# Low words of the weights converted on GpSimd in the first batch

## The chip, the core and the metric

The kernel runs on one core of a Trainium2 chip. A core has five engines with queues of their own: TensorE (PE, the matrix products; PEld is its loading of weights), VectorE (DVE), ScalarE (ACT), GpSimd (POOL) and SyncE (SP, which here only starts transfers). They wait for each other through semaphores. Products go to PSUM, everything else lies in SBUF. The metric is the time of one execution on the device, in microseconds (us), the median of several runs.

## The reference

A two-sided attention between 512 tokens `x` and 32 states `state`, for 8 batches and 8 heads of depth 64, and behind it a two-layer network over the 4,352 rows that come out of it:

```python
scores = scale * x @ state^T;       a  = softmax(scores)    # over the 32 states
xread  = a @ state
scores2 = scale * state @ x^T;      a2 = softmax(scores2)   # over the 512 tokens
sread  = a2 @ x
y = concatenate([xread, sread], axis=2)       # (8, 8, 544, 64), then as rows of 512
h = y @ w_in                                  # 512 -> 2048
g = where(h >= 1, h, where(h <= -1, 0, (h + 1)**2 / 4))
out = g @ w_out                               # 2048 -> 512
```

## The kernel before

**Precision.** Large products run in a reduced fp32 type, so each operand is split into a high and a low part and a product is three passes of PE (high by high, low by high, high by low: lines 477 to 479 and 534 to 536). The weights are laid out by the caller in pieces of 1 MB: eight of `w_in` (called i0 to i7) and eight of `w_out` (o0 to o7). In the core's memory a piece is a tile of 128 x 1024 pairs of 32-bit words, a low word and a high word side by side (`raw_i`, `raw_o`). Three steps make a float of a pair: `high` (line 588, always ACT) converts the high words in place, `low` (lines 575 and 580) the low words in place, and `join` (line 596, always DVE) shifts one and ors the other in. The join of a piece of `w_in` gives `w32_c` (w in the profile). The join of a piece of `w_out` gives `wf`, of which `part_high` (line 603, ACT) and `part_low` (line 607, DVE) make the two parts `wo`.

**Work of a batch.** For a batch: the scores (line 253) into PSUM, `sc`; the softmax over states on DVE and ACT (transposes at line 260, maximum 271, subtraction 275, exponential 280, sum 284, division 288 to 293, transpose back 300), split into `ath` and `atl`; the softmax over tokens (maximum 318, exponential 322 into `e`), its transposes on PE (line 333, `e2p`), the copy of them back by ACT (line 337) and `sread` (line 350, `sr`, scaled into `rs`, then turned by PE in line 364 into `rt`). Since `xread` only feeds `w_in`, the states are multiplied into `w_in` first: `sw` (line 417) of a piece of `w_in`, split by ACT (line 432, `sw_h`) and DVE (line 436, `sw_l`). A block j of 256 hidden values is then `h` (lines 477 to 479), relu by ACT (482), square (485), a bound by DVE (488), its split into `gh` (497, ACT) and `gl` (502, DVE), and the accumulation into `acc` with piece j of `w_out` (lines 534 to 536). Eight blocks make a batch; after eight batches the states' own rows follow.

**Order.** From the second batch on the code is written in the order in which it is to run. The first batch is different: all weights have still to be loaded and converted in it, beside its own products. Its steps go to a planner, `Plan`, as `op(key, engine, cost, run, after, take, ends)`: what a step costs on an engine, what it comes behind, which buffer it takes or frees. `Plan.times` plays the steps through with these costs, the step with the longest way to the end first, and `emit` writes them out in the order in which they then began. So a cost is no more than a number that sets the order. A step whose engine reads "ACT/DVE" goes where it would end sooner. `LATE` is how long after a step's end another engine may see it. Where PE would idle between the first scores and the first accumulation, `emit` puts in warming products (`warm`, line 198) of the identity by itself; `WARM` of them stand ahead of the first scores. Each weight product of 128 x 128 in full fp32 shows as two records in the trace.

**Buffers.** Two `raw` tiles serve all pieces of `w_in` (a piece's transfer waits for the join of the piece two before), while each piece of `w_out` has a tile. One PSUM tile, `mm`, serves `sw`, `e2p`, `sr` and `rt` in turn; one tile `u` holds a block's hidden values until `gl` is made. For the first batch, xt is loaded, and its scores are made, in two halves of 256 tokens, with the state's first slice on ACT's queue beside it. SP's queue holds, in this order: xt of batch 0, i0, i1, o0, the other states, xn of batch 0, i2, o1, xt of batch 1, i3, o2, and so on.

Of the kernel before, what the change touches and what calls it, by code (L numbers as in the profile page):

```python
# [14 lines left out]
AX = mybir.AxisListType  # L15
PSUM = bass.MemoryType.PSUM

WARM = 10
PAD = 120
BIAS = {}  # L20

# [1 line left out]
class Plan:  # L23
# [1 line left out]

    LATE = {"SP": 3.9, "PE": 0.3, "ACT": 0.12, "DVE": 0.12}

    def __init__(self, room, turns, bias):  # L30
        self.bias = bias
# [5 lines left out]
    def op(self, key, engine, cost, run, after=(), take=(), ends=()):  # L37

        after = list(after)
        prior = self.last.get(engine) if engine in ("PE", "SP") else None  # L40
        self.last[engine] = key
        self.ops[key] = [engine, cost, run, after, list(take), list(ends), prior]

    def late(self, k):
        return self.LATE[self.ops[k][0].split("/")[0]]

# [32 lines left out]
    def times(self):  # L79
# [6 lines left out]
        free = dict(self.room)  # L86
        begun, done, where, idle = {}, {}, {}, {e: 0.0 for e in self.LATE}
        events = set()
# [49 lines left out]
def state_exchange_moe(  # L138
# [17 lines left out]
    nc = tc.nc  # L156
# [38 lines left out]
    def warm(n):  # L195

        for _ in range(n):
            nc.tensor.matmul(warmed[:, :P], lhsT=ident, rhs=ident, start=True, stop=True)  # L198
# [254 lines left out]
    class Hidden:  # L453
# [39 lines left out]
        def high(self):  # L493
            b, j = self.b, self.j
            gh = work.tile([P, 2, S], F32R, tag="gh", name=f"gh{b}_{j}")
            gl = work.tile([P, 2, S], F32R, tag="gl", name=f"gl{b}_{j}")
            nc.scalar.copy(out=gh, in_=self.u)  # L497
            gs[b, j] = (gh, gl)

        def low(self):  # L500
            gh, gl = gs[self.b, self.j]
            nc.vector.tensor_tensor(out=gl, in0=self.u, in1=gh.bitcast(F32), op=ALU.subtract)  # L502
# [68 lines left out]
    def low(kind, c, engine):  # L571

        lo = raws[kind, c][..., 0]
        if engine == "DVE":
            nc.vector.tensor_scalar(
                out=lo, in0=lo.bitcast(U32), scalar1=0.875 * 2.0 ** -29, scalar2=0.49,
                op0=ALU.mult, op1=ALU.add,
            )
        else:
            nc.scalar.activation(  # L580
                out=lo, in_=lo.bitcast(U32), func=AF.Relu, scale=0.875 * 2.0 ** -29, bias=offset
            )
# [7 lines left out]
    def join(kind, c):  # L590
        raw = raws[kind, c]
        if kind == "i":
            a = w32[c].rearrange("p k f -> p (k f)")
        else:
            a = parts[c] = work.tile([P, 1024], F32, tag="tmp", name=f"wf{c}")
        nc.vector.scalar_tensor_tensor(  # L596
            out=a.bitcast(I32), in0=raw[..., 1], scalar=3, in1=raw[..., 0],
            op0=ALU.logical_shift_left, op1=ALU.bitwise_or,
        )

    def part_high(c):
        wo[c] = wop.tile([P, 2, 2, DM], F32R, tag="wo", name=f"wo{c}")
        nc.scalar.copy(out=wo[c][:, 0].rearrange("p a c -> p (a c)"), in_=parts[c])  # L603

    def part_low(c):
        wh, wl = (wo[c][:, i].rearrange("p a c -> p (a c)") for i in range(2))
        nc.vector.tensor_tensor(out=wl, in0=parts[c], in1=wh.bitcast(F32), op=ALU.subtract)  # L607
# [5 lines left out]
    op = plan.op  # L613

    def read(key, cost, f, *a, take=(), after=()):
        op(("dma",) + key, "SP", cost, lambda: f(*a), after=after, take=take)

    def load(key, f, b):
        loaded[key, b] = f(b)

    def chunk_ops(c):

        k = ("i", c)
        read(k, 2.6, fetch, "i", c, take=[("raw", k)])
        op(("high",) + k, "ACT", 1.05, lambda: high("i", c), [("dma",) + k])
        op(("low",) + k, "ACT/DVE", (1.15, 0.75), lambda e: low("i", c, e), [("dma",) + k])
        op(("w", c), "DVE", 1.14, lambda: join("i", c), [("high",) + k, ("low",) + k], ends=[k])

    def out_ops(c):

        k = ("o", c)
        read(k, 2.6, fetch, "o", c)
        op(("high",) + k, "ACT", 1.05, lambda: high("o", c), [("dma",) + k])
        op(("low",) + k, "ACT/DVE", (1.15, 0.75), lambda e: low("o", c, e), [("dma",) + k])
        op(("join", c), "DVE", 1.14, lambda: join("o", c), [("high",) + k, ("low",) + k], take=[("tmp", k)])
        op(("woh", c), "ACT", 0.95, lambda: part_high(c), [("join", c)], ends=[k])
        op(("wol", c), "DVE", 1.14, lambda: part_low(c), [("woh", c)], ends=[k])
# [63 lines left out]
    def tensor(key, cost, f, after=(), take=(), ends=()):  # L701
        op(key, "PE", cost, f, after, take, ends)
# [31 lines left out]
    guard = tc.manual_schedule()  # L734
    nc.scalar.dma_start(out=sb[:, 0], in_=state[:, 0])
    read(("xt", 0, 0), 1.3, load, "xt", load_xt, 0, take=[("xt", ("xt", 0))])
    read(("xt", 0, 1), 1.3, lambda: None)
    chunk_ops(0)
    chunk_ops(1)
    out_ops(0)  # L740
    read(("sb", 1), 1.2, lambda: nc.sync.dma_start(out=sb[:, 1:], in_=state[:, 1:]))
    read(("xn", 0), 2.6, load, "xn", load_xn, 0, take=[("xn", ("xn", 0))])
    chunk_ops(2)
    out_ops(1)
    read(("xt", 1), 2.6, load, "xt", load_xt, 1, take=[("xt", ("xt", 1))])
    for c in range(3, NC):
        chunk_ops(c)
        out_ops(c - 1)
        if c == 5:
            read(("xn", 1), 2.6, load, "xn", load_xn, 1, take=[("xn", ("xn", 1))])  # L750
    out_ops(NC - 1)

    op(("table",), "ACT", 1.3, lambda: nc.scalar.copy(out=pad[:, :1], in_=half))
    tensor(("warm",), 4.5, lambda: warm(WARM))
    for side in range(2):
# [113 lines left out]
```

## Time and profile before

| | |
|---|---|
| median of 3 runs | 663.77 us (663.58 to 663.95) |
| span of the profiled execution | 662.2 us; the median of the runs is 1.6 us above it |
| PE busy | 653.9 us, 99% of the span |
| weight loads | 514.2 us, 78% |
| DVE | 340.3 us, 51% |
| ACT | 356.5 us, 54% |
| GpSimd | 0.8 us, seven instructions at the start |
| transfers | 43.65 MB, most of the weights' in the first 60 us |

The page has no other time of the profiled execution than its span. Busy time of PE is no measure of how near it is to its peak, since products overlap; what counts is where it waits. DVE, ACT and the transfers are busiest in the first batch, up to some 95 us, so stretches of it are read one by one.

### The profile page before, as it was taken

The page shows a single profiled execution, that of the slowest core. Times are in us where ns is not written, and L with a number is a line of the kernel's source. Part 1 is how long each engine was busy: PE and PEld are TensorE (multiplying, and loading weights), DVE is VectorE, ACT ScalarE, POOL GpSimd, SP SyncE. Part 2 cuts the span into 40 slices and gives each one's busy share as a digit, 9 for nine tenths or more (in the row PEclk, how much of TensorE's full clock was granted, in tenths as well). Part 3 has the DMA queues.
Part 4 walks back from the last instruction along what each step waited for, and adds up shares of the span by engine and source line. Part 5 has one row for each costly group of instructions (what it writes and reads, how often), then busy time and mean ns, then how long its engine had stood idle before and what let it go on. Part 6 is the DMA issues. An engine that isn't in the chain of part 4 may idle for free.

```text
span 662.2 us, 10304 instructions
## 1 busy us (share of the span) xinstructions
PE 653.9 (99%) x4442; PEld 514.2 (78%) x4442; DVE 340.3 (51%) x490; ACT 356.5 (54%) x462; POOL 0.8 (0%) x7
## 2 busy tenths in 40 slices
PE   8999999999999999999999999999999999999997
PEld 6677777777787777777787777777778777778896
DVE  5999947623673239433563338433563343333431
ACT  4899847544554446544554447444653454454642
POOL 0000000000000000000000000000000000000000
PEclk9999999999999999999999999999999999999999
DMA  8986103010301003010301002010100000000101
GB/s 359 400 359 249 64 10 119 0 65 0 120 10 64 1 4 124 0 65 0 128 1 64 1 24 105 0 65 0 65 1 1 1 33 32 1 1 1 63 1 33
DMA packets 11085, 43.65 MB, mean 66 GB/s; under 512 B 1312, under 2 KB 1440, under 8 KB 7968
## 3 DMA queue, kind: packets, MB, share of 16 engines
q1 hardware_dynamic: 6096, 34.28, 13.6%
q10 hardware_dynamic: 4944, 8.72, 3.5%
q8 instruction: 35, 0.57, 0.3%
q14 instruction: 10, 0.08, 0.0%
HBM read 34.08 MB, written 8.91 MB: 65 GB/s over the span
## 4 chain that ended last, share of the span: by engine, by line
PE 91%; ACT 5%; DVE 3%; issue 0%; DMA 0%; POOL 0%; SPq 0%; ACTq 0%; POOLq 0%
PE acc L534 19%; PE acc L536 18%; PE acc L535 18%; PE h L477 9%; PE h L479 9%; PE h L478 9%; PE sw L417 5%; PE sc L253 1%; PE sr L350 1%; PE e2p L333 1%; PE warmed L198 1%; ACT u L482 1%; ACT u L485 1%; ACT raw_i L588 1%; DVE w L596 1%; ACT wo L603 0%
## 5 line engine op out<-in xcount | busy, mean ns | idle before, releaser
L534 PE MATMUL acc<-wo,gh 128*128 128x512 f32 x544 | 218.8, 402 | 0.0
L535 PE MATMUL acc<-wo,gh 128*128 128x512 f32 x544 | 212.3, 390 | 0.0
L536 PE MATMUL acc<-wo,gl 128*128 128x512 f32 x544 | 212.2, 390 | 0.0
L482 ACT ACTIVATE u<-h,half 128x512 f32<-128x512 f32 x136 | 93.7, 693 | 219.9 <-PE h L479 202.6
L488 DVE SCALAR_TENSOR_TENSOR u<-u,h 128x512 f32<-128x512 f32 x136 | 87.0, 680 | 206.7 <-ACT u L485 206.7
L534 PEld LDWEIGHTS acc<-wo,gh 128*128 128x128 f32 x544 | 102.1, 188 | 40.1 <-ACT u L482 12.8
L536 PEld LDWEIGHTS acc<-wo,gl 128*128 128x128 f32 x544 | 102.1, 188 | 22.5 <-issue 0.4
L535 PEld LDWEIGHTS acc<-wo,gh 128*128 128x128 f32 x544 | 102.2, 188 | 19.4 <-DVE wo L607 0.3
L502 DVE TENSOR_TENSOR gl<-u,gh 128x1024 fp32r<-128x1024 f32 x68 | 83.2, 1224 | 33.0 <-ACT gh L497 32.0
L497 ACT CAST gh<-u 128x1024 fp32r<-128x1024 f32 x68 | 71.8, 1056 | 50.3 <-DVE u L488 49.9
L485 ACT ACTIVATE u<-u 128x1024 f32<-128x1024 f32 x68 | 72.5, 1065 | 1.3
L417 PE MATMUL sw<-w,sb 64*32 64x256 f32 x1024 | 36.0, 383 | 1.8 <-DVE w L596 1.3
L417 PEld LDWEIGHTS sw<-w,sb 64*32 64x32 f32 x1024 | 15.1, 106 | 17.9 <-issue 8.8
L479 PE MATMUL h<-atl,sw_0h 128*128 128x512 f32 x60 | 23.6, 393 | 0.3 <-DVE atl L306 0.2
L477 PE MATMUL h<-ath,sw_0h 128*128 128x512 f32 x60 | 23.5, 394 | 0.0
L549 ACT COPY o<-acc 128x512 f32<-128x512 f32 x33 | 18.6, 586 | 9.1 <-PE acc L536 9.0
L478 PE MATMUL h<-ath,sw_0l 128*128 128x512 f32 x60 | 23.5, 391 | 0.0
L479 PE MATMUL h<-atl,sw_6h 128*128 128x512 f32 x60 | 23.4, 389 | 0.0
L479 PE MATMUL h<-atl,sw_2h 128*128 128x512 f32 x60 | 23.4, 389 | 0.0
L477 PE MATMUL h<-ath,sw_2h 128*128 128x512 f32 x60 | 23.3, 389 | 0.0
L478 PE MATMUL h<-ath,sw_2l 128*128 128x512 f32 x60 | 23.3, 389 | 0.0
L477 PE MATMUL h<-ath,sw_4h 128*128 128x512 f32 x60 | 23.3, 389 | 0.0
(174 smaller groups left out, 735.0 us busy)
## 6 DMA issues: line engine op xcount, KB each, us to landing
xt<-in_xt_dram SPq DMA_DIRECT2D x16, 512.0 KB, 4.5
raw_i<-in_moe_w_in_dram SPq DMA_DIRECT2D x8, 1024.0 KB, 6.9
raw_o<-in_moe_w_out_dram SPq DMA_DIRECT2D x8, 1024.0 KB, 9.4
xn<-in_x_dram SPq DMA_DIRECT2D x8, 1024.0 KB, 6.4
out_dram<-o ACTq DMA_DIRECT2D x32, 256.0 KB, 2.0
sb<-in_state_dram SPq DMA_DIRECT2D x1, 448.0 KB, 12.6
out_dram<-o SPq DMA_DIRECT2D x4, 64.0 KB, 1.7
out_dram<-o ACTq DMA_DIRECT2D x4, 64.0 KB, 2.0
```

The source lines that it names most:

```text
L417: nc.tensor.matmul(pt[pr * NS:(pr + 1) * NS, hh, i * CI:(i + 1) * CI], lhsT=sb[rows, b, pr], rhs=w32[c + i][rows, pr], start=True, stop=True,)
L477: nc.tensor.matmul(o, lhsT=wh[:, k, sl], rhs=ah[:, k], start=first, stop=False)
L478: nc.tensor.matmul(o, lhsT=wl[:, k, sl], rhs=ah[:, k], start=False, stop=False)
L479: nc.tensor.matmul(o, lhsT=wh[:, k, sl], rhs=al[:, k], start=False, stop=last)
L482: nc.scalar.activation(out=self.u[:, i], in_=self.hs[i], func=AF.Relu, scale=0.5, bias=half)
L485: nc.scalar.activation(out=self.u, in_=self.u, func=AF.Square)
L488: nc.vector.scalar_tensor_tensor(out=self.u[:, i], in0=self.u[:, i], scalar=1.0, in1=self.hs[i], op0=ALU.min, op1=ALU.max,)
L497: nc.scalar.copy(out=gh, in_=self.u)
L502: nc.vector.tensor_tensor(out=gl, in0=self.u, in1=gh.bitcast(F32), op=ALU.subtract)
L534: nc.tensor.matmul(a, lhsT=lh, rhs=oh, start=f == 0, stop=False)
L535: nc.tensor.matmul(a, lhsT=lh, rhs=ol, start=False, stop=False)
L536: nc.tensor.matmul(a, lhsT=ll, rhs=oh, start=False, stop=f == NF - 1)
```

## The change

The low words of i2 to i7 and o2 to o7 are converted by GpSimd, with the instruction that DVE used; those of i0, i1, o0 and o1 stay with ACT or DVE. The planner is told 1.7 for such a step, and 0.2 as GpSimd's delay. Eight warming products stand ahead of the first scores instead of ten, and the planner takes the second half of xt to be there 0.6 earlier.

```diff
-WARM = 10
+WARM = 8
...
-    LATE = {"SP": 3.9, "PE": 0.3, "ACT": 0.12, "DVE": 0.12}
+    LATE = {"SP": 3.9, "PE": 0.3, "ACT": 0.12, "DVE": 0.12, "POOL": 0.2}
...
         lo = raws[kind, c][..., 0]
-        if engine == "DVE":
-            nc.vector.tensor_scalar(
+        if engine != "ACT":
+            (nc.vector if engine == "DVE" else nc.gpsimd).tensor_scalar(
                 out=lo, in0=lo.bitcast(U32), scalar1=0.875 * 2.0 ** -29, scalar2=0.49,
                 op0=ALU.mult, op1=ALU.add,
             )
...
+    def low_op(kind, c):
+        k = (kind, c)
+        if c < 2:
+            op(("low",) + k, "ACT/DVE", (1.15, 0.75), lambda e: low(kind, c, e), [("dma",) + k])
+        else:
+            op(("low",) + k, "POOL", 1.7, lambda: low(kind, c, "POOL"), [("dma",) + k])
...
-        op(("low",) + k, "ACT/DVE", (1.15, 0.75), lambda e: low("i", c, e), [("dma",) + k])
+        low_op("i", c)
...
-        op(("low",) + k, "ACT/DVE", (1.15, 0.75), lambda e: low("o", c, e), [("dma",) + k])
+        low_op("o", c)
...
-    read(("xt", 0, 1), 1.3, lambda: None)
+    read(("xt", 0, 1), 0.7, lambda: None)
```

The planner orders the first batch anew. On PE the order of products stays, and the numbers of warming products change: 8 instead of 10 ahead of the first scores, none instead of 2 between the halves of the scores, 18 instead of 16 behind them, 10 instead of 8 ahead of the transposes `e2p` of batch 0.

Three places follow; in each, the row in brackets names the engines that an instruction waits for. First DVE, around the first scores. Before (`sc0_0` and `sc0_1` are the two halves of the heads, `z0` the transposed scores; the first two transposes are those of the first 256 tokens, the other two those of the second 256):

```order
L260 STREAM_TRANSPOSE z0_120<-sc0_0_118 128x256 [waits PE_49]
L260 STREAM_TRANSPOSE z0_120<-sc0_1_119 128x256 [waits PE_49]
L271 TENSOR_REDUCE m1_0_121<-z0_120 128x8 [waits DVE_49] x2
L260 STREAM_TRANSPOSE z0_120<-sc0_0_118 128x256 [waits PE_49]
L260 STREAM_TRANSPOSE z0_120<-sc0_1_119 128x256 [waits PE_49]
L271 TENSOR_REDUCE m1_0_121<-z0_120 128x8 [waits DVE_49] x2
L275 TENSOR_TENSOR z0_120<-z0_120,m1_0_121 128x512 [waits DVE_49]
```

DVE at the same place in the changed kernel:

```order
L260 STREAM_TRANSPOSE z0_118<-sc0_0_116 128x256 [waits PE_49]
L260 STREAM_TRANSPOSE z0_118<-sc0_1_117 128x256 [waits PE_49]
L260 STREAM_TRANSPOSE z0_118<-sc0_0_116 128x256
L271 TENSOR_REDUCE m1_0_119<-z0_118 128x8 [waits DVE_49] x2
L260 STREAM_TRANSPOSE z0_118<-sc0_1_117 128x256
L275 TENSOR_TENSOR z0_118<-z0_118,m1_0_119 128x512 [waits DVE_49]
L271 TENSOR_REDUCE m1_0_119<-z0_118 128x8
L271 TENSOR_REDUCE m1_0_119<-z0_118 128x8 [waits DVE_49]
```

The third transpose has moved ahead of the maxima, and the transposes of the second half have no wait for PE of their own any more.

Second ACT, from the second split of the first softmax to the copy of the turned exponentials. Before (`ath0` is the split, `e2_0` the exponentials over tokens, `u0_0` and `h0_0` block 0 of batch 0, `sw0_1h` the high part of sw 1):

```order
L303 CAST ath0_116<-zt0_200 128x512 [waits DVE_49]
L322 ACTIVATE e2_0_237,sum2_0_239<-sc0_0_118,nm2_0_238 128x512 [waits DVE_49,Activation_49]
L482 ACTIVATE u0_0_222<-h0_0_0_223,half_78 128x512 [waits PE_49]
L482 ACTIVATE u0_0_222<-h0_0_1_229,half_78 128x512 [waits PE_49]
L432 CAST sw0_1h_262<-sw0_1_253 128x512 [waits PE_49]
L485 ACTIVATE u0_0_222<-u0_0_222 128x1024 [waits Activation_49]
L322 ACTIVATE e2_0_237,sum2_0_239<-sc0_1_119,nm2_0_238 128x512 [waits DVE_49]
L588 ACTIVATE raw_i2_198<-raw_i2_198 128x1024 [waits DMAHW0_49]
L497 CAST gh0_0_306<-u0_0_222 128x1024 [waits DVE_49,Activation_49]
L603 CAST wo0_310<-wf0_247 128x1024
L337 COPY e2_0_237<-e2p0_286 128x1024 [waits PE_49,Activation_49]
```

ACT there in the changed kernel:

```order
L303 CAST ath0_114<-zt0_198 128x512 [waits DVE_49]
L588 ACTIVATE raw_i2_192<-raw_i2_192 128x1024 [waits DMAHW0_49,Activation_49]
L482 ACTIVATE u0_0_220<-h0_0_0_221,half_78 128x512 [waits PE_49]
L482 ACTIVATE u0_0_220<-h0_0_1_227,half_78 128x512 [waits PE_49]
L432 CAST sw0_1h_261<-sw0_1_252 128x512 [waits PE_49]
L485 ACTIVATE u0_0_220<-u0_0_220 128x1024 [waits Activation_49]
L322 ACTIVATE e2_0_235,sum2_0_237<-sc0_0_116,nm2_0_236 128x512 [waits DVE_49]
L322 ACTIVATE e2_0_235,sum2_0_237<-sc0_1_117,nm2_0_236 128x512 [waits DVE_49]
L603 CAST wo0_279<-wf0_247 128x1024
L497 CAST gh0_0_301<-u0_0_220 128x1024 [waits DVE_49,Activation_49]
L337 COPY e2_0_235<-e2p0_292 128x1024 [waits PE_49,Activation_49]
```

The high words of i2 have moved from behind the second exponential to the front, and the first exponential from the front to behind the square. On DVE the join of i2 now stands where its low conversion stood, ahead of `sw0_1l`, and the low part of o0 (line 607) ahead of `gl` of block 0.

Third ACT at block 3 of batch 0, from `gh` of block 2 to the square. Before (`e2_1` are the exponentials of batch 1, `u0_3` block 3, `sw0_4h` the high part of sw 4):

```order
L497 CAST gh0_2_529<-u0_2_424 128x1024 [waits DVE_49,Activation_49]
L322 ACTIVATE e2_1_517,sum2_1_519<-sc1_487,nm2_1_518 128x512 [waits DVE_49,PE_49]
L322 ACTIVATE e2_1_517,sum2_1_519<-sc1_487,nm2_1_518 128x512 [waits DVE_49]
L588 ACTIVATE raw_o4_436<-raw_o4_436 128x1024 [waits DMAHW1_49]
L482 ACTIVATE u0_3_532<-h0_3_0_533,half_78 128x512 [waits DVE_49,PE_49,Activation_49]
L432 CAST sw0_4h_562<-sw0_4_553 128x512 [waits PE_49]
L482 ACTIVATE u0_3_532<-h0_3_1_543,half_78 128x512
L588 ACTIVATE raw_i6_499<-raw_i6_499 128x1024 [waits DMAHW3_49]
L485 ACTIVATE u0_3_532<-u0_3_532 128x1024 [waits Activation_49]
```

ACT there in the changed kernel:

```order
L497 CAST gh0_2_510<-u0_2_428 128x1024 [waits DVE_49,Activation_49]
L588 ACTIVATE raw_o4_440<-raw_o4_440 128x1024 [waits DMAHW1_49]
L322 ACTIVATE e2_1_525,sum2_1_527<-sc1_494,nm2_1_526 128x512 [waits DVE_49,PE_49]
L322 ACTIVATE e2_1_525,sum2_1_527<-sc1_494,nm2_1_526 128x512 [waits DVE_49]
L482 ACTIVATE u0_3_537<-h0_3_0_538,half_78 128x512 [waits DVE_49,PE_49,Activation_49]
L588 ACTIVATE raw_i6_489<-raw_i6_489 128x1024 [waits DMAHW3_49,Pool_49]
L482 ACTIVATE u0_3_537<-h0_3_1_550,half_78 128x512 [waits PE_49]
L432 CAST sw0_4h_570<-sw0_4_561 128x512 [waits PE_49]
L485 ACTIVATE u0_3_537<-u0_3_537 128x1024 [waits Activation_49]
```

The cast of sw 4 now stands behind i6's high words and the second relu, and o4's high words have moved ahead of the exponentials. GpSimd's queue holds the twelve conversions in the order i2, i3, o2, i4, o3, i5, o4, i6, o5, i7, o6, o7, each waiting for its transfer. SP's order is the same up to o5; xt of batch 2, which stood ahead of i7, now stands behind o7.

## The prediction

> **What bounds the kernel now.** I read the stretches first (columns: stretch, length, busy time of PE, PEld, DVE, ACT and POOL, granted clock, DMA share, GB/s), then TensorE's list of waits, then the timeline around the places that these name.
>
> ```profile
> 13.00:20.00 7.00, 6.13 (x50) 4.58 (x50) 6.93 (x14) 5.65 (x7) 0.00 (x0) 1.00 1.02 416
> 20.00:30.00 10.00, 8.85 (x74) 6.07 (x73) 9.62 (x16) 8.85 (x14) 0.00 (x0) 1.00 0.98 397
> 30.00:40.00 10.00, 10.00 (x116) 7.53 (x115) 9.73 (x13) 10.00 (x12) 0.00 (x0) 1.00 0.83 315
> 40.00:50.00 10.00, 9.98 (x72) 6.86 (x68) 9.03 (x14) 9.19 (x14) 0.00 (x0) 1.00 1.00 420
> 50.00:60.00 10.00, 10.00 (x70) 7.32 (x71) 9.62 (x12) 10.00 (x13) 0.00 (x0) 1.00 0.97 377
> 60.00:70.00 10.00, 9.86 (x61) 7.39 (x59) 9.96 (x15) 10.00 (x13) 0.00 (x0) 1.00 0.05 20
> ```
>
> From 30 us on PE has next to no idle time, and nothing behind the first batch is touched: the time is the moment at which the first batch hands over, plus fixed work. Ahead of 30 us PE waits. There DVE works 6.93 of 7.00 and 9.62 of 10.00 us, the transfers run at a share of 1.02 and 0.98, and from 30 to 70 us DVE and ACT are both nearly full. So this is a chain through DVE, ACT and transfers up to 30 us, and a race that PE only just wins up to 70 us. GpSimd does nothing.
>
> ```profile
> PE sw L417 <- DVE w L596: 1.3, 1, 1.3
> ```
>
> This is the longest wait of PE behind its start, and warming products fill most of the rest; a gain there must come from the chain that the fillers cover.
>
> **The scores (two warming products less).**
>
> ```profile
> 0.73 0.42 ACTq L735 DMA_DIRECT2D sb<-in_state_dram  x1
> 0.74 0.87 SPq L217 DMA_DIRECT2D xt<-in_xt_dram  x2
> 1.45 4.34 PEld L198 LDWEIGHTS warmed<-ident 128*128 128x128 f32 x20 [1.45 <-POOL ident masks.py:199]
> 6.01 1.11 PE L253 MATMUL sc<-xt,sb 64*32 64x256 f32 x16
> 7.21 0.78 DVE L260 STREAM_TRANSPOSE z<-sc 128x256 f32<-128x256 f32 x2 [6.31 <-PE sc L253]
> 7.73 0.97 PE L253 MATMUL sc<-xt,sb 64*32 64x256 f32 x16
> 8.04 0.18 PEld L253 LDWEIGHTS sc<-xt,sb 64*32 64x32 f32 x14 [0.18 <-DVE z L260]
> 8.78 0.78 DVE L260 STREAM_TRANSPOSE z<-sc 128x256 f32<-128x256 f32 x2 [0.16 <-PE sc L253]
> 10.11 0.68 DVE L275 TENSOR_TENSOR z<-z,m 128x512 f32<-128x512 f32 x1
> DMA to landing us min/median/max: 4.3/4.3/4.3
> DMA to landing us min/median/max: 4.2/4.6/5.0
> ```
>
> Twenty weight loads, two to a product, take 4.34 us: 0.43 a product, 0.87 for two. The first half of the scores could start at 6.01 - 0.87 = 5.14. The state lands at 0.73 + 4.3 = 5.03, the first half of xt at 0.74 + 4.2 = 4.94, so that holds. The half takes 7.05 - 6.01 = 1.04 (the four fillers behind it begin at 7.05, 0.16 ahead of the transposes at 7.21) and ends at 6.2, when the second half of xt lands (issued at about 1.2, 5.0 later). The two fillers between the halves are gone too. Before, the second half waited for the first transposes (row at 8.04); now it follows at once and ends at 7.24.
>
> But DVE's order (shown above for both) has the transposes of the first half wait for PE and those of the second half for nothing: the one wait covers both halves. They start 0.16 behind the second half, at 7.40. The eight instructions ahead of the first subtraction then run without the gap of 0.16: 10.11 - 7.21 - 0.16 = 2.74, up to 10.14 against 10.11. **Term: 0.0.** Bounds: -0.75, if the transposes start behind the first half, at 6.4, and keep a gap; +0.2, if the second half of xt lands that much later. After that DVE has the same instructions up to the first join of w_out, so sw and the softmax of batch 0 stay where they are.
>
> **Piece 2 of w_in, and what stands behind it on ACT.**
>
> ```profile
> 13.79 0.33 SPq L568 DMA_DIRECT2D raw_i<-in_moe_w_in_dram  x1
> DMA to landing us min/median/max: 6.8/6.8/6.8
> 21.15 0.69 ACT L322 ACTIVATE e<-sc,nm 128x512 f32<-128x512 f32 x1 [1.94 <-DVE nm L319]
> 21.83 1.26 ACT L482 ACTIVATE u<-h,half 128x512 f32<-128x512 f32 x2
> 23.60 0.69 DVE L436 TENSOR_TENSOR sw_1l<-sw,sw_1h 128x512 fp32r<-128x512 f32 x1
> 24.39 0.70 ACT L322 ACTIVATE e<-sc,nm 128x512 f32<-128x512 f32 x1
> 25.06 1.20 ACT L588 ACTIVATE raw_i<-raw_i 128x1024 f32<-128x1024 f32 x1
> 25.24 0.66 PE L333 MATMUL e2p<-ident,e 128*128 128x128 f32 x4 [0.24 <-ACT e L322]
> ```
>
> Piece 2 is issued at 13.79 and lands 6.8 later, at 20.6; with a DMA share of 1.02 it can't land earlier. ACT's conversion of its high words (1.20, of which the next instruction overlaps some 0.1) stood behind both second exponentials; it now stands ahead of the relus of block 0 and waits for that landing: 20.6 to 21.7. The relus started at 21.83, behind an exponential that had waited 1.94 for DVE: no loss. But both exponentials now come behind relus, cast and square. From 21.83 to 24.39 is 2.56, so the first starts at 24.26, the second 0.68 later (21.15 to 21.83), at 24.94, where it stood at 24.39. PE's second half of the transposes, 25.24 before, and block 1 behind it come 0.55 later.
>
> ```profile
> 27.99 1.04 ACT L337 COPY e<-e2p 128x1024 f32<-128x1024 f32 x1
> 29.09 0.67 PE L417 MATMUL sw<-w,sb 64*32 64x256 f32 x16 [0.45 <-ACT e L337]
> 30.17 0.19 PEld L535 LDWEIGHTS acc<-wo,gh 128*128 128x128 f32 x1 [0.30 <-DVE wo L607]
> ```
>
> That loss is covered: behind block 1 PE waited 0.45 for ACT's copy of the turned exponentials, and then 0.30 for the low part of w_out 0. The copy started 3.60 behind the second exponential (24.39 to 27.99); one conversion, 1.1, has left that stretch, so it starts at 24.94 + 3.60 - 1.1 = 27.44, and 0.55 earlier than before. The product sw_2 starts at 29.09 - 0.45 + 0.55 = 29.2 (+0.1). The low part of w_out 0 now stands ahead of gl on DVE, so the 0.30 goes; some of it may come back as a wait for gl, so I keep a **term of -0.2**. Bounds: -0.75, if the exponentials aren't later and both waits go; +0.55, if nothing covers.
>
> GpSimd's first conversion has to be over before DVE's join of piece 2, which stands ahead of sw_1l:
>
> ```profile
> 1.10 0.29 POOL masks.py:199 TENSOR_SCALAR_AFFINE_SELECT ident<-ident 128x128 f32<-128x128 f32 x1
> L575 DVE TENSOR_SCALAR raw_i<-raw_i x6: 684/686/690, 10.7 to 61.5; 128x1024 int32<-128x1024 uint32 x6
> ```
>
> No row has GpSimd on such a tile. Its select over 128 elements took 0.29; eight times that, 2.3, is the upper bound, DVE's 0.69 for the same instruction the lower. I take 1.7, nearer the row of its own engine. The Trainium skill ("GPSIMD Engine Reference", section 7) has about 1.9 cycles an element for such strides, an estimate of 1.6 us at 1.2 GHz; no run here shows it, and the sum would be the same. From 20.65 it ends at 22.4. DVE comes to the join at 23.60 - 0.69 = 22.9, where its own low conversion stood, spends 1.2 on it, and sw_1l ends at 24.7: still ahead of the first exponential's end at 24.95. **Term: 0**, cover 0.25 us.
>
> **Relief, and a new stall.** Seven conversions of 0.69 leave DVE (nine before, two left) and five leave ACT. PE hardly waits from 30 to 60 us, so by themselves they are worth nothing. One place gets worse, ACT's order at block 3:
>
> ```profile
> 48.98 1.18 DVE L502 TENSOR_TENSOR gl<-u,gh 128x1024 fp32r<-128x1024 f32 x1
> 50.82 0.70 ACT L482 ACTIVATE u<-h,half 128x512 f32<-128x512 f32 x1
> 51.40 0.61 ACT L432 CAST sw_4h<-sw 128x512 fp32r<-128x512 f32 x1
> 52.35 0.68 DVE L436 TENSOR_TENSOR sw_4l<-sw,sw_4h 128x512 fp32r<-128x512 f32 x1
> 53.39 0.27 PE L364 MATMUL rt<-ident,rs 128*128 128x128 f32 x1
> ```
>
> PE reaches rt at 53.39 and needs the buffer that sw_4l frees at 52.35 + 0.68 = 53.03: a margin of 0.36. ACT's cast sw_4h stood straight behind the first relu; now that relu, piece 6's high words (1.1) and the second relu (0.58, as 50.82 to 51.40) are ahead of it, 1.7 later. The first relu itself comes earlier: it needs gl, over at 50.16, and a conversion that held it until 50.82 has moved ahead of the exponentials: -0.65. Net 1.05 late: **+0.7** behind the margin (bounds 0 and +1.3). A like order stands at block 4, where PE idles 0.14 between 60 and 70 us now; 0 to 1.1, and I take **+0.1**, since ACT has been relieved by then. On SP's queue xt of batch 2 goes behind i7, o6 and o7; it is used after the first batch, the transfers end near 60 us (share 0.05 behind it): nothing, and the three pieces come earlier.
>
> **Sum.** 0.0 - 0.2 + 0.7 + 0.1 = +0.6. The profiled span is 662.2 us, 1.6 below the runs' median of 663.77; I add the difference to the median: **664.4 us**. About 0.2% (1.3 us) is what a measurement of this kernel can tell from no change, so this is no change. Its own range: 663.2 to 665.4.
>
> **Rivals.**
>
> 1. *DVE and GpSimd hinder each other: slower.* DVE's busiest groups between 28 and 62 us:
>
> ```profile
> L596 DVE SCALAR_TENSOR_TENSOR wf<-raw_o 128x1024 int32<-128x1024 int32 x5 | 6.1, 1217 | 0.0
> L607 DVE TENSOR_TENSOR wo<-wf,wo 128x1024 fp32r<-128x1024 f32 x5 | 6.1, 1214 | 0.0
> L596 DVE SCALAR_TENSOR_TENSOR w<-raw_i 128x1024 int32<-128x1024 int32 x4 | 4.9, 1217 | 0.0
> L502 DVE TENSOR_TENSOR gl<-u,gh 128x1024 fp32r<-128x1024 f32 x4 | 4.8, 1210 | 0.0
> ```
>
> Eighteen instructions with two SBUF inputs take 21.9 of 34 us, and eleven of the twelve GpSimd conversions fall here. A GpSimd instruction of 1.7 us always meets one. If each stops DVE for half its length, DVE loses 11 x 0.85 = 9.4 us, gets back 6 x 0.69 = 4.1 (those of the seven that stood here) and has 1.6 idle from 30 to 60 us: 3.7 late, and PE with it, its margin at rt being 0.36: 668.1. At full length it is 18.7 - 5.7 = 13.0, 677.4. It decides from a loss of 0.5 us for each conversion. For it: DVE is full and can absorb nothing. Against: ACT and DVE run side by side on these tiles, and DVE's instructions keep their length (1210 to 1217 ns) beside a full ACT. The Trainium skill ("SBUF — State Buffer", "Who interferes with whom") makes it a rule: a vector instruction with two SBUF inputs and a GpSimd instruction that reads SBUF exclude each other, and the second is blocked until the first ends. No row here can test it, since POOL is idle. By that rule the time lies between the two ends above. Chance 0.34.
>
> 2. *GpSimd becomes the bound: slower.* From 20.6 to about 60 us (the DMA share is 0.05 behind it) there are 3.3 us for each of twelve conversions. At 4 us each they end 8 us late: 672. Only a GpSimd slower than eight times its 0.29 would do that. Chance 0.10.
>
> 3. *The early start carries: faster.* The transposes start with the first half (-0.75), both waits of PE ahead of 30 us go (-0.75), and the rest is absorbed: 662.3. Against it stands the order of DVE's waits. Chance 0.12.
>
> **Numbers.** Forecast 0.44. Faster is rival 3 (0.12), same the forecast (0.44), slower rivals 1 and 2 (0.44). The range 662.6 to 673 leaves out most of rival 3 and the far end of rival 1, 0.2 in all.
>
> **What would show it.** First transposes of DVE at 7.4, first subtraction near 10.1: the first term. ACT's high words of piece 2 from 20.6 to 21.7 and sw_2 at 29.2: the second. A wait of PE before rt near 53 us for sw_4l: the third. If DVE's two-input rows stretch towards 2 us while POOL is busy, or gaps that no engine explains stand before them, rival 1 holds; GpSimd rows far above 2.3 us make rival 2; transposes at 6.4, rival 3. The forecast is wrong if these move the time by more than 1.3 us.

## Result and profile after

The changed kernel takes **670.84 us** (median of 4 runs, 670.64 to 671.99) against 663.77 before (663.58 to 663.95): 7.07 us more, ratio 1.0114 [1.0100, 1.0127]. The prediction was 664.4, no change; its range of 662.6 to 673.0 holds the result, and its rival 1 (DVE and GpSimd hinder each other, 668.1 to 677.4) is what happened.

The profiled execution took 670.71 us with a span of 668.9, against 662.2 before: a difference of 6.7. Before, only two waits of TensorE in the first 100 us were longer than 0.5: the one at the start (1.4) and the one for w (1.3). Now these are (engine, line, what it waited for; sum, times, longest):

```profile
PE sc L253 <- DVE sw_3l L436: 2.7, 1, 2.7
PE sw L417 <- DVE w L596: 2.2, 1, 2.2
PE warmed L198 <- POOL ident masks.py:199: 1.5, 1, 1.5
PE e2p L333 <- DVE u L488: 1.3, 1, 1.3
PE e2p L333 <- DVE sw_5l L436: 1.3, 1, 1.3
PE rt L364 <- DVE sw_4l L436: 1.1, 1, 1.1
```

Four of them are new. The one for u lies at 25 us and belongs to the new order (the write-only run below has it too, 1.3). Those for sw_3l, sw_4l and sw_5l lie between 43 and 70 us, where PE had won its race by a margin of 0.36 at rt. DVE is who is late. The stretches of after, in the columns that the prediction's first view has:

```profile
30.00:40.00 10.00, 10.00 (x116) 7.35 (x115) 9.00 (x11) 8.78 (x10) 4.35 (x3) 1.00 0.72 273
40.00:50.00 10.00, 7.33 (x49) 4.74 (x36) 9.53 (x11) 8.02 (x10) 4.12 (x3) 0.84 1.01 414
50.00:60.00 10.00, 8.92 (x52) 6.42 (x52) 9.50 (x11) 6.92 (x11) 3.99 (x3) 0.99 0.68 257
60.00:70.00 10.00, 8.66 (x53) 6.32 (x52) 10.00 (x10) 9.00 (x12) 1.23 (x1) 1.00 0.39 157
```

DVE stays as busy as before while it does less: 43 instructions from 30 to 70 us where there were 54 (13, 14, 12 and 15). So on average each takes longer. In part that is because short conversions have left; the groups from 20 to 70 us by shape (after the bar: busy time, mean ns of one) show the other part:

```profile
L596 DVE SCALAR_TENSOR_TENSOR wf<-raw_o 128x1024 int32<-128x1024 int32 x7 | 10.3, 1473 | 0.0
L607 DVE TENSOR_TENSOR wo<-wf,wo 128x1024 fp32r<-128x1024 f32 x6 | 9.1, 1519 | 0.4 <-ACT wo L603 0.4
L502 DVE TENSOR_TENSOR gl<-u,gh 128x1024 fp32r<-128x1024 f32 x4 | 7.4, 1858 | 0.0
L596 DVE SCALAR_TENSOR_TENSOR w<-raw_i 128x1024 int32<-128x1024 int32 x6 | 7.3, 1216 | 0.2 <-POOL raw_i L575 0.2
L488 DVE SCALAR_TENSOR_TENSOR u<-u,h 128x512 f32<-128x512 f32 x9 | 5.8, 678 | 0.4 <-ACT u L485 0.3
L575 POOL TENSOR_SCALAR raw_o<-raw_o 128x1024 int32<-128x1024 uint32 x6 | 8.5, 1416 | 9.4 <-DMA raw_o<-in_moe_w_out_dram 9.4
L575 POOL TENSOR_SCALAR raw_i<-raw_i 128x1024 int32<-128x1024 uint32 x6 | 7.9, 1323 | 36.0 <-DMA raw_i<-in_moe_w_in_dram 29.8 <-DVE r L339 5.6 <-DVE sw_2l L436 0.6
```

L596 for w_out (wf), L607 and L502 read two operands from SBUF; their means rose from 1217, 1214 and 1210 ns to 1473, 1519 and 1858. L488, which reads one operand from PSUM, keeps its length (681 before). L596 for w_in (w) also reads two from SBUF and keeps its 1216: none of these joins began while GpSimd was converting. Instruction by instruction, around the second GpSimd conversion (GpSimd's rows, then DVE's; start, length):

```profile
28.05 1.13 POOL L575 TENSOR_SCALAR raw_i<-raw_i 128x1024 int32<-128x1024 uint32 x1 [5.62 <-DVE r L339]
30.38 1.98 POOL L575 TENSOR_SCALAR raw_o<-raw_o 128x1024 int32<-128x1024 uint32 x1 [1.21 <-DMA raw_o<-in_moe_w_out_dram]
...
28.12 2.12 DVE L502 TENSOR_TENSOR gl<-u,gh 128x1024 fp32r<-128x1024 f32 x1
30.16 1.21 DVE L596 SCALAR_TENSOR_TENSOR wf<-raw_o 128x1024 int32<-128x1024 int32 x1
```

GpSimd begins at 28.05 and ends at 29.18. DVE's gl starts 0.07 behind it and takes 2.12: what is left of GpSimd's 1.13 (1.06), then its own 1.21, would be 2.27, and the row is 0.15 shorter. At 30.16 DVE comes first, keeps its 1.21, and GpSimd's next conversion stretches to 1.98 instead. Whoever begins first runs at full speed, the other stands. The Trainium skill ("SBUF — State Buffer", "Who interferes with whom") says just that of a DVE instruction with two SBUF inputs and a GpSimd instruction that reads SBUF, and the trace agrees. Seven DVE rows are of this kind, 1.98 to 2.13 us long, the first at 28.12 (above) and the last at 62.19; together they are 6.2 us over seven times 1.21.

### The profile page after: what moved, and what is told of

Same layout as the page of the kernel before. It is cut to its first block, busy times and chain, and to the rows that moved or that the text cites. A ratio compares the mean times of both kernels' runs of the same rounds, so it can differ in the third digit from the quotient of the medians.

```text
span 668.9 us, 10322 instructions
## 1 busy us (share of the span) xinstructions
PE 654.3 (98%) x4442; PEld 514.7 (77%) x4442; DVE 342.4 (51%) x483; ACT 352.2 (53%) x457; POOL 17.3 (3%) x19
## 3 DMA queue, kind: packets, MB, share of 16 engines
q10 hardware_dynamic: 4944, 8.72, 3.5%
## 4 chain that ended last, share of the span: by engine, by line
PE 91%; ACT 3%; DVE 3%; DMA 1%; issue 1%; POOL 0%; SPq 0%; ACTq 0%; DVEq 0%; POOLq 0%
PE acc L534 19%; PE acc L536 18%; PE acc L535 18%; PE h L477 9%; PE h L479 9%; PE h L478 9%; PE sw L417 4%; PE sc L253 1%; DMA raw_i<-in_moe_w_in_dram 1%; PE sr L350 1%; PE e2p L333 1%; ACT raw_i L588 1%; ACT raw_o L588 1%; DVE wo L607 1%; DVE wf L596 1%; PE warmed L198 1%
## 5 line engine op out<-in xcount | busy, mean ns | idle before, releaser
L488 DVE SCALAR_TENSOR_TENSOR u<-u,h 128x512 f32<-128x512 f32 x136 | 86.9, 680 | 206.9 <-ACT u L485 206.7
L502 DVE TENSOR_TENSOR gl<-u,gh 128x1024 fp32r<-128x1024 f32 x68 | 85.8, 1262 | 34.5 <-ACT gh L497 33.5
L479 PE MATMUL h<-atl,sw_0h 128*128 128x512 f32 x60 | 23.6, 393 | 0.3 <-DVE atl L306 0.2
L478 PE MATMUL h<-ath,sw_4l 128*128 128x512 f32 x60 | 23.4, 389 | 0.0
```

The costliest lines, as they stand in the source:

```text
L478: nc.tensor.matmul(o, lhsT=wl[:, k, sl], rhs=ah[:, k], start=False, stop=False)
L479: nc.tensor.matmul(o, lhsT=wh[:, k, sl], rhs=al[:, k], start=False, stop=last)
L488: nc.vector.scalar_tensor_tensor(out=self.u[:, i], in0=self.u[:, i], scalar=1.0, in1=self.hs[i], op0=ALU.min, op1=ALU.max,)
```

## Experiments

Ten kernels, each timed against the kernel before on the same chip (663.55 for the first four, 663.65 for the next four, 663.33 for the last two).

| kernel | median us (runs) | ratio to before |
|---|---|---|
| early start alone | 665.09 (10) | 1.0023 [1.0014, 1.0033] |
| GpSimd alone | 670.35 (4) | 1.0092 [1.0075, 1.0109] |
| GpSimd on 8 columns | 665.51 (8) | 1.0027 [1.0016, 1.0038] |
| GpSimd only writes | 665.03 (7) | 1.0024 [1.0013, 1.0035] |
| fewer fillers alone | 662.89 (11) | 0.9990 [0.9981, 0.9999] |
| one piece on GpSimd | 663.14 (11) | 0.9993 [0.9984, 1.0002] |
| two pieces on GpSimd | 663.22 (11) | 0.9992 [0.9983, 1.0001] |
| changed, with products in the wait | 670.53 (4) | 1.0105 [1.0091, 1.0118] |
| before, with a bystander on GpSimd | 670.66 (4) | 1.0110 [1.0093, 1.0127] |
| changed, with the old cost | 667.84 (4) | 1.0068 [1.0053, 1.0083] |

One of the four executions of GpSimd alone took 2293 us; it is in the median of 670.35 (670.23 without it), not in the ratio.

**Is it GpSimd's hold on SBUF, or the order?** In the first kernel all low words stay with ACT and DVE:

```diff
-        if c < 2:
+        if True:
             op(("low",) + k, "ACT/DVE", (1.15, 0.75), ...
```

> Eight warming products and the earlier second half of the scores alone; every low-word conversion stays with ACT and DVE. Theory A (the two engines exclude each other at SBUF): the 6.7 us behind 28 us of the changed kernel are all GpSimd's, so this runs at 663.8 give or take 0.8, with the first subtraction of the softmax near 8.7 us as in the changed kernel and no DVE instruction with two inputs above 1.25 us. Theory B (the early start reorders the first batch for the worse): over 667.

665.09: neither. The two edits of the early start cost 1.5 us by themselves, less than B's 667 and more than A's 664.6. The fifth run takes that apart.

The second has the conversions without the early start:

```diff
-WARM = 8
+WARM = 10
-    read(("xt", 0, 1), 0.7, lambda: None)
+    read(("xt", 0, 1), 1.3, lambda: None)
```

> GpSimd's twelve conversions alone; ten warming products and the order of the scores as before. Theory A: DVE's two-input instructions stretch to about 2.1 us wherever GpSimd begins just ahead of them; the early start is worth nothing behind 29 us, so the time is that of the changed kernel, 670.8 give or take 1.5. Theory B: under 666.

670.35: A. Its other three executions lie at 668.56 (under A's bound of 669.3), 670.23 and 670.47, with mean granted clocks of 1.0, 0.997 and 0.997; I come back to that.

The third and fourth keep the changed kernel's order and alter only what GpSimd does in it:

```diff
         lo = raws[kind, c][..., 0]
+        if engine == "POOL":
+            lo = lo[:, :8]
...
-            ..., scalar=3, in1=raw[..., 0],
+            ..., scalar=3, in1=raw[..., 0] if c < 2 else zeros.broadcast_to([P, 1024]),
```

> The changed kernel's order on every engine, but each GpSimd conversion covers 8 of its 1024 columns, and the joins of those pieces take a column of zeros as their low words (the low words of pieces 2 to 7 are left out). The joins still read 1024 elements from SBUF. Theory A (length of GpSimd's hold on SBUF): DVE's two-input instructions go back to 1.21 us, PE's waits of 2.7, 1.1 and 1.3 us for sw_3l, sw_4l and sw_5l go, and the time is 670.8 - 2.75 - 1.45 - 1.2 - 1.2 = 664.2, give or take 1. Theory C (the new order of ACT and DVE costs it, as the prediction's third term had it): stays above 668.

```diff
         lo = raws[kind, c][..., 0]
+        if engine == "POOL":
+            nc.gpsimd.memset(lo, 0)
+            return
```

> The changed kernel's order, but GpSimd fills the low words of its twelve pieces with zeros in place of converting them (a write without a read; the low words of pieces 2 to 7 are left out). Joins wait for GpSimd as in the changed kernel. Theory A1 (only a GpSimd instruction that reads SBUF holds DVE off): DVE's two-input instructions stay at 1.21 us, 664 give or take 1. Theory A2 (any GpSimd access does, for its length): instructions stretch by the length of a fill, about 0.9 us each if the fill takes 1.1, and the time is 669 to 671.

665.51 and 665.03, each just above the bounds that theory A set (665.2 and 665). Every engine's order is that of the changed kernel in both, and they lie 2.0 and 1.5 above their own kernel before: so at most that much of the 7.1 us is order. The rest, 5.1 and 5.6, goes when GpSimd stops reading 1024 columns. The fill is the cleaner of the two, since it lasts as long as the conversion and stands at the same place. Its rows beside gl, and its groups:

```profile
28.18 1.05 POOL L575 MEMSET raw_i<- 128x1024 int32 x1 [6.27 <-DVE r L339]
...
28.22 1.21 DVE L502 TENSOR_TENSOR gl<-u,gh 128x1024 fp32r<-128x1024 f32 x1
```

```profile
L610 DVE TENSOR_TENSOR wo<-wf,wo 128x1024 fp32r<-128x1024 f32 x7 | 8.5, 1219 | 0.4 <-ACT wo L606 0.4
L502 DVE TENSOR_TENSOR gl<-u,gh 128x1024 fp32r<-128x1024 f32 x5 | 6.0, 1208 | 0.0
```

gl starts 0.04 us behind a fill of 1.05 and still takes 1.21, where the conversion made it 2.12. So A1: writing doesn't hold DVE, reading does. The section of the skill named above says so too (not with a GpSimd instruction that only writes).

**A neighbour for whom nobody waits.** The ninth kernel leaves the program before as it is on PE, DVE, ACT and SP, and lets the idle GpSimd look at data:

```diff
+        if c > 1:
+            op(("look", c), "POOL", 2.4, lambda: look(c), [("w", c)])
...
+    def look(c):
+        for _ in range(2):
+            nc.gpsimd.tensor_scalar(out=seen, in0=w32[c]..., scalar1=1.0, scalar2=0.0, ...)
```

> The kernel before, its order on PE, DVE, ACT and SP untouched. GpSimd, idle there, reads each finished w_in tile of pieces 2 to 7 twice (128x1024 float32 into a tile that nobody uses): twelve instructions for which nobody waits, straight behind DVE's joins. Theory A (a GpSimd instruction that reads SBUF and a DVE instruction with two SBUF inputs exclude each other): six to twelve of DVE's instructions stretch by up to 0.9 us; DVE, which keeps all its conversions, falls 4 to 9 us behind, and the time is 667 to 672. Theory C (the changed kernel lost by waits for GpSimd's results and by its order): 663.7 give or take 0.4.

670.66, 7.3 us more than before, from twelve instructions that deliver nothing to anyone; in its profile no engine waits for them. Theory A holds with no help from order or waits. DVE's rows show also whom else it hits:

```profile
27.14 3.08 POOL L605 TENSOR_SCALAR seen<-w 128x1024 uint8<-128x1024 f32 x2 [25.73 <-DVE w L596]
...
28.10 1.01 DVE L339 TENSOR_SCALAR r<-sum 128x2 f32<-128x2 f32 x1
...
29.23 2.06 DVE L616 TENSOR_TENSOR wo<-wf,wo 128x1024 fp32r<-128x1024 f32 x1
...
39.19 1.33 DVE L575 TENSOR_SCALAR raw_i<-raw_i 128x1024 int32<-128x1024 uint32 x1
```

L575 has one SBUF input and 0.68 us of its own, and takes 1.33 here; L339 works on two elements and takes 1.01 for 0.16. Both are tensor_scalar from SBUF to SBUF. Two inputs are thus not the whole condition; the same section of the skill counts tensor_scalar among the operations that can take the shared ports, and the trace agrees.

**What cost the early start its gain?** The fifth kernel drops the two fillers and leaves the planner's cost of the second half of the tokens at 1.3, so that only the fillers change and all other work keeps its order:

```diff
-WARM = 10
+WARM = 8
```

> The kernel before with eight warming products instead of ten and nothing else: the planner's cost of the second half of the tokens stays at 1.3, so every other engine keeps the order of before. Theory P (in the run with the early start alone it was the planner's cost, which set ACT's conversion of piece 2 between the two exponentials, that cost 1.5 us; fewer fillers are a gain): the first subtraction at 9.3, block 1 some 0.7 us earlier than before, the time 662.9, between 662.4 and 663.3. Theory Q (fewer fillers are themselves the loss, by the clock that drops in the longer wait): 664.5 or more.

662.89, theory P's number, and 0.76 faster than before: less than the 1.3 us that count as told apart, though its interval ends below 1. P's steps were less exact than its sum: in the profiled execution (662.42) the first subtraction stands at 8.52, not 9.3, and block 1 comes 1.6 earlier, not 0.7. Against the early start alone (665.09) the difference is one number of the planner, worth 2.3 us when each run is set against its own kernel before. By the product sw_0 this kernel is 1.0 ahead (12.19 against 13.18): 0.3 by the start of its scores in the profiled execution, the rest because DVE's transposes of the first half don't wait for the second. ACT's second exponential of batch 0 makes it 2.1. First the kernel with the cost of 0.7, then this one:

```profile
20.62 1.18 ACT L588 ACTIVATE raw_i<-raw_i 128x1024 f32<-128x1024 f32 x1 [2.00 <-DMA raw_i<-in_moe_w_in_dram]
24.92 0.71 ACT L322 ACTIVATE e<-sc,nm 128x512 f32<-128x512 f32 x1
```

```profile
22.81 0.70 ACT L322 ACTIVATE e<-sc,nm 128x512 f32<-128x512 f32 x1
23.47 1.20 ACT L588 ACTIVATE raw_i<-raw_i 128x1024 f32<-128x1024 f32 x1
```

At 0.7 ACT stands for 2.0 us waiting for piece 2, with the exponentials behind; at 1.3 it does them first, and piece 2 can wait. The planner, told that data come sooner than they do, put waits for data ahead of work that was ready.

**The four corners.** The tenth kernel completes a square (all with eight fillers):

```diff
-    read(("xt", 0, 1), 0.7, lambda: None)
+    read(("xt", 0, 1), 1.3, lambda: None)
```

> The whole change but for the planner's cost of the second half of the tokens, which stays at 1.3: the order of the run with GpSimd alone, with eight warming products. If DVE's lateness by contention sets the hand-over (5.8 us of it, measured against the run in which GpSimd only writes) and the earlier start is a gain of 0.76 that DVE carries on: 670.35 - 0.76 = 669.6, give or take 0.8. If the planner's cost were what contention acts through: under 667.

| | cost 1.3 | cost 0.7 |
|---|---|---|
| low words on ACT and DVE | 662.89 | 665.09 |
| twelve on GpSimd | 667.84 | 670.84 (the change) |

667.84, 1.8 under the expected 669.6 and outside its bounds: the sum started from the median of GpSimd alone, where the clock was below 1 in two executions; from the one at 1.0 (668.56) it is 667.8, but that is a reading made afterwards. Why that kernel falls into two groups was not found. The four corners were not all timed on one chip; each against the kernel before on its own, they stand at -0.76, +1.54, +4.51 and +7.07. So GpSimd costs 5.3 us at the old cost and 5.5 at the new, the planner's number 2.3 and 2.6: the two add up within 0.3 us, and the fillers give 0.8 back.

**Is the half clock a part of it?** In the changed kernel the stretch from 40 to 50 us has a granted clock of 0.84 (above), right behind PE's wait of 2.7 us, and I had counted some 1.4 us for products at half speed. The eighth run keeps PE busy in that wait:

```diff
-        2: ... lambda: att_start(1), ...
+        2: ... lambda: (add_zeros(10), att_start(1)), ...
```

> The changed kernel, with ten products of a tile of zeros added to the accumulator ahead of the scores of batch 1, where PE waits 2.7 us for sw_3l. Theory H (the half clock from 47.0 to 49.8 comes of that wait): products of 0.23 behind it, mean granted clock 1.0, and 1.4 us less: 669.4 give or take 0.4. Theory K (the clock is granted by something else, such as the load on all engines): the clock stays below 1 and the time at 670.8 give or take 0.4.

670.53: K's number, though not by K's reason. Its rows for 40 to 50 and 60 to 70 us, and the wait before rt:

```profile
40.00:50.00 10.00, 9.46 (x76) 7.04 (x61) 9.87 (x11) 7.70 (x10) 3.93 (x3) 1.00 1.02 416
...
60.00:70.00 10.00, 10.00 (x54) 7.50 (x53) 10.00 (x11) 8.74 (x12) 1.86 (x1) 0.88 0.30 121
```

```profile
PE rt L371 <- DVE sw_4l L443: 2.1, 1, 2.1
```

The clock is full where it was 0.84, so that half of H is right, and PE is 1.2 us earlier at block 3. But it then waits 2.1 at rt instead of 1.1, and the half clock comes behind that wait (0.88 in the last stretch). What ties the runs together is when DVE begins sw_5l (last two figures ahead of the semicolon: first and last start), in the kernel before, the changed one, the one that only writes, and this one:

```profile
L436 DVE TENSOR_TENSOR sw_5l<-sw,sw_5h x1: 681/681/681, 62.1 to 62.1; 128x512 fp32r<-128x512 f32 x1
```

```profile
L436 DVE TENSOR_TENSOR sw_5l<-sw,sw_5h x1: 672/672/672, 68.8 to 68.8; 128x512 fp32r<-128x512 f32 x1
```

```profile
L436 DVE TENSOR_TENSOR sw_5l<-sw,sw_5h x1: 682/682/682, 63.0 to 63.0; 128x512 fp32r<-128x512 f32 x1
```

```profile
L443 DVE TENSOR_TENSOR sw_5l<-sw,sw_5h x1: 675/675/675, 68.9 to 68.9; 128x512 fp32r<-128x512 f32 x1
```

6.7 of lateness on DVE is the 6.7 of the span, and it is 6.8 here with another history on PE. In the write-only run it is 0.9. That profiled execution is the longest of its kernel (666.71, the others 664.71 to 665.40), with a granted clock of 0.95 throughout, so its span can't be set against the others; but the run on 8 columns, with a clock of 1.0 from 20 us on, agrees: sw_5l starts at 63.3, 1.2 late, and the span is 1.5 longer. The new bound is DVE. The half clock is a small part at most, as far as one execution shows it: of the four of this eighth run one had a mean clock of 1.0 and took 670.03, the others, at 0.995 to 0.997, took 670.44 to 670.90. In GpSimd alone the lower clock goes with 1.7 to 1.9 us more; there is no trace of such an execution, so what the clock costs there stays open. It is not needed for the effect: the tenth run, at 0.999 to 1.0 in all four executions, still lies 4.5 us above its kernel before.

**How much GpSimd is free?** The sixth and seventh runs are the fewer-fillers kernel with one and two of the conversions on GpSimd (the planner is told 1.2 for them instead of 1.7):

```diff
-        if c < 2:
+        if not (k == ("o", 2)):     # the other: if not (c == 2):
```

> As the run with fewer fillers alone, and GpSimd converts the low words of one piece, number 2 of w_out, and no other. If contention is paid for each conversion that meets a two-input instruction of DVE, one conversion costs at most 0.9 us and gives back 0.69 on DVE or ACT: 662.5, between 662.2 and 663.6. If a GpSimd that works at all costs the kernel its microseconds, 666 or more.

> As the run before, with two conversions on GpSimd: piece 2 of w_in and piece 2 of w_out. Contention by the piece: 662.5, between 662.2 and 664.5 (both conversions may meet a two-input instruction, 0.9 each). A GpSimd that costs as a whole: 666 or more.

663.14 and 663.22: within 0.4 of the kernel without any, and not better. In both DVE's instructions with two SBUF inputs keep means of 1.21 to 1.22 us: these conversions (1.14 in the one, 1.27 and 1.31 in the other) met nobody or came second. Contention is paid by the meeting, not for a GpSimd that works; and the relief of ACT and DVE bought nothing here. No kernel tried was faster than two fillers less and nothing else.

## Why the prediction was wrong, step by step

**The step that failed** is the missing term: the sum 0.0 - 0.2 + 0.7 + 0.1 has none for GpSimd beside DVE. The effect stood in the text as rival 1 with 0.34, held down by one row: DVE keeps its length beside a full ACT. That row is of another pair of engines. Before the change GpSimd was idle, so no row could speak on this pair; what did was the rule of the skill, quoted there, and it gave the sign. It should have been the forecast. What the runs showed in its place is a term of 5.1 to 5.6 us, with DVE's two-input instructions at 1.98 to 2.13 us instead of 1.21 wherever GpSimd had begun to read first. The range of 662.6 to 673 holds 670.84 only because it was drawn to take in the near part of rival 1; the forecast's own range ended at 665.4, and its sign of being wrong, a move of more than 1.3 us with rows near 2 us, came true.

**Rival 1's size.** It took 11 meetings at half of 1.7 us, 9.4, less 5.7 of relief and idle time: 3.7 at the low end. Both terms were off, to opposite sides, so that the result lies between its two ends is in part luck. GpSimd's conversion was shorter (1.12 to 1.13 undisturbed), and seven of the twelve held a DVE instruction, for 0.9 each: 6.2, not 9.4. But the 5.7 did not come back (see the relief below). So the point from which it decides, 0.5 us for each conversion, was wrong: the loss was 6.2 / 12 = 0.52, which by that sum would have left the time 0.5 later, not 5 to 6.

**Scores, term 0.0.** The rows of after:

```profile
5.17 1.45 PE L253 MATMUL sc<-xt,sb 64*32 64x256 f32 x32
...
6.71 1.11 DVE L260 STREAM_TRANSPOSE z<-sc 128x256 f32<-128x256 f32 x3 [5.81 <-PE sc L253]
8.36 0.44 DVE L260 STREAM_TRANSPOSE z<-sc 128x256 f32<-128x256 f32 x1
8.72 0.65 DVE L275 TENSOR_TENSOR z<-z,m 128x512 f32<-128x512 f32 x1
```

One wait covers both halves, as said. But the halves in one go take 1.45, not twice 1.04, so the transposes start at 6.71 (7.40 forecast); and six instructions, not eight, stand ahead of the first subtraction, as the order already showed: 8.72, not 10.14. The product sw_0 came 0.76 earlier (13.77 to 13.01), as much as rival 3 had for the scores, though by another way; it was gone by 29 us.

**Piece 2, term -0.2.** Right in its steps:

```profile
20.65 1.18 ACT L588 ACTIVATE raw_i<-raw_i 128x1024 f32<-128x1024 f32 x1 [2.20 <-DMA raw_i<-in_moe_w_in_dram]
24.96 0.69 ACT L322 ACTIVATE e<-sc,nm 128x512 f32<-128x512 f32 x1
27.52 1.02 ACT L337 COPY e<-e2p 128x1024 f32<-128x1024 f32 x1
29.11 0.66 PE L417 MATMUL sw<-w,sb 64*32 64x256 f32 x16
```

Forecast were 20.6, 24.94, 27.44 and 29.2. What the term didn't see is that the early start would have been kept but for this order, as the fifth run keeps it (sw_2 at 27.50): the wait of 2.20 for the landing took it. GpSimd's conversion, forecast to cost nothing here, did: DVE's join waited 0.24 for it.

**rt +0.7, block 4 +0.1.** PE did wait for sw_4l, behind ACT's late cast, but in the changed kernel this drowned in DVE's lateness. It can be read from the write-only run, whose order is the same: PE is 0.4 us late at rt against before (53.77 for 53.39) and another 0.5 at the transposes of batch 1's exponentials (the run on 8 columns, at a full clock there, has 0.6 and 0.6). So 0.9 to 1.2 against a forecast of 0.8, and the whole order 1.5 us against 0.6. Without contention the forecast would have missed by 0.9.

**Relief worth nothing:** right. The write-only run has all of it and, at 665.03, is no faster than the early start alone (665.09), which has none. DVE's work shows where it went. From the start of sw_1l (23.6 in all three) to that of sw_5l DVE is busy for 36.6 us before and for 36.7 in the write-only run, although six conversions, 4.1 us, have left that stretch: the planner has moved other work into it, one more join and low part of w_out and two maxima of batch 1 among it. In the changed kernel it is busy for 42.7 us there: the stretching came on top, with nothing to absorb it.

## What to carry over

Before work goes to an idle engine, ask which ports its instructions share with the engine that is to be relieved, and count how often the two will meet: here 4.8 us of conversions were taken off DVE, and 6.2 us of standing still came back. A row that shows two engines side by side speaks for those two alone. And a planner's cost is a claim about time: one that is too low for a transfer puts a wait ahead of ready work, here at a price of 2.3 to 2.6 us, which undid a gain of 0.8.

## What the hardware showed that I had not expected

- GpSimd's conversion of 128x1024 took 1.12 to 1.13 us alone, two thirds of my 1.7, and of the 1.6 estimated from the Trainium skill ("GPSIMD Engine Reference", section 7). On 8 columns it took 0.20 where it met nobody and up to 1.24 where it began beside a DVE instruction with two SBUF inputs, which kept its 1.22.
- The half clock comes sooner than I had thought. In the kernel with the early start alone PE waited 2.2 us ahead of sw_0, and its stretch reads:

```profile
PE sw L417 <- DVE w L596: 2.2, 1, 2.2
```

```profile
10.00:15.00 5.00, 2.79 (x28) 1.79 (x27) 4.93 (x12) 3.70 (x6) 0.00 (x0) 0.81 1.02 426
```

The changed kernel has the same wait of 2.2 and a clock of 1.0 there, so it is not sure to come. The Trainium skill ("TensorE: Matmul & The Clock Gate") puts the drop at an idle window of about 3.4 us; these waits are shorter. In the ten runs of that kernel it made no difference to the time, whether the mean clock was 0.996 or 1.0 (664.8 to 665.4); in the profiled one the product behind that wait took 1.11 us, and 3.0 us of warming products followed.
